# Attention keys by head, and first scores on 64-row, 32-column tiles of the array

## The chip, the cores and the metric

The kernel runs on one core of a Trainium2 chip. The metric is the device time of one execution in microseconds. Before the change its median was 1553.74 us over three runs (1549.90 to 1557.67). TensorE (PE) multiplies and transposes through a 128x128 array into PSUM (eight banks of 512 f32 columns); VectorE (DVE) and ScalarE (ACT) move and compute; SyncE (SP) and GpSimd (POOL) issue DMA.

## The reference

Three stages follow each other, over 8 batches, 8 heads, 576 tokens and a head size of 64, with 32 packed queries `p` per head:

```
p_packed = softmax(scale * p @ k.T) @ v          # first scores: 32 x 576 per head
out      = softmax(scale * q @ p_packed.T) @ p_packed
x        = heads side by side (8, 576, 512)
r, k     = sigmoid(xr @ w_r), relu(xk @ w_k) ** 2 # xr, xk: x mixed with the token before
x2       = r * (k @ w_v)
u        = x2 + (x2.T @ U @ V).T
result   = u + relu(u @ w_ch1) @ w_ch2
```

The change is in `p @ k.T`, the loads of `k` and the layouts around it.

## The kernel before

**Units.** Attention is cut into 16 units: a pair of batches (`b2` = 0, 1) times a pair of heads (`h` = 0, 1). `attention_steps` (line 634) builds one unit. A unit's keys are 2 x 576 tokens for each of two heads. `load_k` (line 591) brings, for each batch, the first 512 tokens as 128 partitions of four tokens (`p t`), and the last 64 tokens of both batches into the last 128 columns of the same tile `kin`. On a partition the order is token, head, feature, so that 128 neighbouring columns are one token of both heads.

**First scores.** Four transposes per batch turn `kin` into `kh` (row = head and feature, column = token), one more handles the tail of both batches. The packed queries of two heads are put side by side with the other head's features zeroed (`pbd`, a product with the mask `hmask`) and transposed to `pT`, so that a contraction over all 128 rows gives both heads' scores: 64 output rows per batch, in two column chunks of 288. Each of the four f32 matmuls has a stationary operand of 128 rows and 64 columns and is two MATMUL passes. The outputs of batch 0 and 1 lie on partitions 0 to 63 and 64 to 127 of one bank; the two chunks have a bank each. Two maxima, an exponential per chunk (and one per batch for the tail), and the transposes of the weights `a1` follow. Its columns are 128 per `t`.

**Order.** No order is written by hand. A planner (class `Plan`, `emit`) collects all operations with their dependencies and simulates a clock: PE and SP take, among what is ready, the lowest class and then the lowest position in the program (line 439); ACT and DVE take the lowest class and then what was ready first. A matmul of n moving columns is priced by line 203 as `f * max(f * n / 2.4, 107.0) + 3.0` ns with f = 2 for f32, whatever its tile, and at twice that where its own count of recent columns (line 202) is low (line 459). A DMA is priced at 358 GB/s if its shortest contiguous run is 512 B or more, else 180 (line 318). Attention is class 0, ahead of the matmuls of the next stages (class 1). The engines then run their queues in this order.

**Stages.** The first four units have buffers of their own, use all eight banks and are interleaved with one another, three steps apart (`LAG`, line 501), together with the casts of the first weights; their loads are issued in the order of `FIRST` (line 502). The other twelve run one after the other between the matmuls of the mixing stage (tiles `psr`, `psk`, `psv`), with two banks. The last stage (tiles `psc`) starts when the mixing stage ends.

Of the kernel before, what the change touches and what calls it, by code (L numbers as in the profile page):

```python
# [9 lines left out]
F32 = mybir.dt.float32  # L10
# [3 lines left out]
AF = mybir.ActivationFunctionType  # L14
ALU = mybir.AluOpType
# [454 lines left out]
def packed_attention_moe_mixer_kernel(  # L470
# [18 lines left out]
    B, H, S, D = q.shape  # L489
    NP = p.shape[2]  # L490
    P = 128
# [12 lines left out]
    SCALE = 1.0 / float(D) ** 0.5  # L504
# [3 lines left out]
    plan = Plan(nc)  # L508
    add, sub, mul = ALU.add, ALU.subtract, ALU.mult
# [22 lines left out]
    def ctile(name, shape, dt=F32):  # L532
        return plan.fixed(const.tile(shape, dt, name=name))

    ident = ctile("ident", [P, P])
    hmask = ctile("hmask", [P, 2, D])
# [8 lines left out]
    def ps_att():  # L545
        return plan.bank(att_banks[0], "psat", att_banks[0] is ps_a)
# [8 lines left out]
    p_t = {}  # L555

    def load_p(bp):
        t = plan.tile(p_p, [P, NJ, D], F32, "p", parts=(0, 1))
        for b2 in range(2):
            plan.dma(t.at(b2)[b2 * 64:(b2 + 1) * 64],  # L560
                     p[2 * bp + b2].rearrange("(j h) k d -> (h k) j d", h=2))
        p_t[bp] = t

    class Bufs:
# [26 lines left out]
        def load_k(self, u, after=()):  # L591
            bp, j = divmod(u, NJ)
            if u not in self.kin:
                self.kin[u] = self.tile_in("kin")
            t = self.kin[u]
            for b2 in range(2):
                src = k[2 * bp + b2, 2 * j:2 * j + 2]
                plan.dma(
                    t.at(b2)[:, b2 * 512:(b2 + 1) * 512].rearrange("p (t h d) -> p t h d", t=4, h=2),
                    src[:, 0:512, :].rearrange("h (p t) d -> p t h d", t=4), after=after)  # L600
            for b2 in range(2):
                src = k[2 * bp + b2, 2 * j:2 * j + 2]
                plan.dma(
                    t.at(2 + b2)[b2 * 64:(b2 + 1) * 64, 1024:1152].rearrange("p (h d) -> p h d", h=2),
                    src[:, 512:576, :].rearrange("h s d -> s h d"), after=after)
# [28 lines left out]
    def attention_steps(A, u, u_next):  # L634
        bp, j = divmod(u, NJ)
        kin, qin, vin = A.kin.pop(u), A.qin.pop(u), A.vin.pop(u)
        if j == 0 and bp + 1 < NBP:
            load_p(bp + 1)
        plan.tt(A.pbd, p_t[bp][:, j, :].unsqueeze(1).to_broadcast([P, 2, D]), hmask, mul)
        plain = u < NPLAIN  # L640
        kh = A.big(F32, "kh")
        qt, at = A.big(F32, "qt"), A.big(F32, "at")
        pT, ppz = A.keep(plain)
# [7 lines left out]

        if u_next is not None:
            A.kin[u_next], A.qin[u_next], A.vin[u_next] = [A.tile_in(n) for n in ("kin", "qin", "vin")]
        for b2 in range(2):
            yield
            ps = ps_att()
            for t in range(4):
                plan.transpose(ps[:, t * P:(t + 1) * P],
                               kin.at(b2)[:, b2 * 512 + t * P:b2 * 512 + (t + 1) * P], ident)
            sl = slice(b2 * 576, b2 * 576 + 512)  # L660
            plan.copy(kh[:, sl], ps)
        yield
        ps = ps_att()
        plan.transpose(ps[:, 0:P], kin[:, 1024:1152], ident)
        plan.transpose(ps[:, P:2 * P], A.pbd.rearrange("p h d -> p (h d)"), ident)
        pk_ = ps[:, 0:P].rearrange("p (b c) -> p b c", b=2)
        pp_ = ps[:, P:2 * P].rearrange("p (b c) -> p b c", b=2)
        khr = kh.rearrange("p (b c) -> p b c", b=2)[:, :, 512:576]
        plan.copy(khr, pk_)
        plan.copy(pT, pp_)  # L670
        if u_next is not None:
            A.load_k(u_next, A.after)

        st = plan.tile(A.one, [P, 16], F32, "st", parts=(0, 1))
        sps = []
        for c in range(2):
            yield
            ps = ps_att()
            for b2 in range(2):
                plan.mm(ps[b2 * 64:(b2 + 1) * 64, 0:288], pT[:, b2, :],  # L680
                        kh[:, b2 * 576 + c * 288:b2 * 576 + (c + 1) * 288],
                        start=True, stop=True, skip_group_check=True)
            plan.reduce(st[:, c:c + 1], ps[:, 0:288], ALU.max)
            sps.append(ps)
        plan.tt(st[:, 2:3], st[:, 0:1], st[:, 1:2], ALU.max)
        plan.ts(st[:, 3:4], st[:, 2:3], -SCALE, None, mul)
        a1 = A.a1
        bias = st.at(0)[:, 3:4]
        plan.act(a1[:, 0:288], sps[0][:, 0:288], AF.Exp, st.at(1)[:, 4:5], bias, SCALE)
        plan.act(a1[:, 288:512], sps[1][:, 0:224], AF.Exp, st.at(1)[:, 5:6], bias, SCALE)  # L690
        for b2 in range(2):
            r = slice(b2 * 64, (b2 + 1) * 64)
            plan.act(a1[r, 512 + b2 * 64:576 + b2 * 64], sps[1][r, 224:288], AF.Exp,
                     st.at(1)[r, 6:7], bias[r], SCALE)
        plan.reduce(st[:, 7:8], st[:, 4:7], add)
        plan.ts(st[:, 8:9], st[:, 7:8], 1e-9, None, add)
# [2 lines left out]
        for c in range(3):  # L699
            yield  # L700
            ps = ps_att()
# [3 lines left out]
            n = 3 if c < 2 else 2  # L705
# [9 lines left out]
        ps = ps_att()  # L715
# [4 lines left out]
        ps = ps_att()  # L720
# [4 lines left out]
        ps = ps_att()  # L725
        vm = vin[:, 0:1024].rearrange("p (b h t d) -> p b h t d", b=2, h=2, t=4)
        for t in range(4):
            for b2 in range(2):
                plan.mm(ps[b2 * 64:(b2 + 1) * 64, 0:P],
                        at[:, t * P + b2 * 64:t * P + (b2 + 1) * 64], vm[:, b2, :, t, :],  # L730
                        start=(t == 0), stop=False, skip_group_check=True)
# [9 lines left out]
        ps = ps_att()  # L741
# [36 lines left out]
        ps = ps_att()  # L778
# [4 lines left out]
        ps = ps_att()  # L783
        plan.transpose(ps[:, 0:P], a2g[:, 512:640], ident)
        for b2 in range(2):
            r = slice(b2 * 64, (b2 + 1) * 64)
            halves(th[r, 512:576], None if plain else tl[r, 512:576], ps[r, r])
        xo = A.big(F32, "xo", (0, 1)).rearrange("p (i b c) -> p i b c", i=NI, b=2)
        for c0, c1 in ((256, 576), (0, 256)):
# [4 lines left out]
            for n, (lh, rh) in enumerate(terms):  # L794
                for b2 in range(2):
                    r = slice(b2 * 64, (b2 + 1) * 64)
                    plan.mm(pss[b2][:, 0:w], ppz[r, lh, :], rh[r, c0:c1], start=(n == 0),
                            stop=(n + 1 == len(terms)))
# [5 lines left out]
    def attention(A, u, u_next):  # L804
        for _ in attention_steps(A, u, u_next):
            pass
# [94 lines left out]
    plan.cls = 0  # L901
    A0.after = go
    steps = [attention_steps(AX_[u], u, NJ if u == 0 else None) for u in range(NJ)]
    step = 0
    while any(s is not None for s in steps):
# [32 lines left out]
    for b2 in range(2):  # L938
        r = slice(b2 * 64, (b2 + 1) * 64)
# [5 lines left out]
    for i0, i1 in ((0, NI),):  # L945
        src = uv[:, i0 * NP:i1 * NP]
# [260 lines left out]
    def product(q, f, i, name, fresh):  # L1207

        if fresh:
            bank_abc[name] = plan.bank(ps_c1, "psc1")  # L1210
        ps = bank_abc[name][:, 0:256]
        w, x = load_ws(f, i), ops[q][i]
        n = 0
        for k in range(2):
            for wi, a in PASS:
                plan.mm(ps, half(w, wi)[:, k * P:(k + 1) * P],
                        half(x, a)[:, k * 256:(k + 1) * 256],
                        start=(fresh and n == 0), stop=(n == 5), skip_group_check=True)
                n += 1
        return ps  # L1220
# [53 lines left out]
    for n in range(len(chunks)):  # L1274
        b, c = chunks[n]
# [27 lines left out]
        if n >= CAST0:  # L1303
            plan.cls = 3
            for _ in range(len(casts) if n == NCAST else NPER):
                if casts:
                    rows, src, size, put = casts.pop(0)
# [27 lines left out]
    for q in range(NQ):  # L1335
# [11 lines left out]
        for f in range(NF):  # L1347
# [7 lines left out]
            b = product(q, f, 1, "b", True)  # L1355
# [4 lines left out]
            c = product(q, f, 2, "c", True)  # L1360
# [66 lines left out]
```

## Time and profile before

| what | value |
|---|---|
| median of three runs | 1553.74 us |
| the profiled execution's own time | 1553.02 us |
| its span, first to last instruction | 1551.2 us |
| mean granted TensorE clock | 0.986 |
| PE, PEld busy | 97%, 85% |
| DVE, ACT, POOL busy | 62%, 45%, 17% |

The times of the rows are of the one profiled execution. A MATMUL's recorded duration contains its way through the array, so that neighbours overlap in the records; how fast matmuls follow each other is read from their starts. PEld is the load of stationary operands, beside PE.

### The profile page before, as it was taken

To read this page: it belongs to the slowest core of one execution; us is meant where nothing else is said; L and a number is where in the kernel's file an instruction comes from. 1 tells how busy PE (TensorE), PEld (TensorE's weight loads), DVE (VectorE), ACT (ScalarE), POOL (GpSimd) and SP (SyncE) were. 2 spreads that over 40 slices of the span, in tenths; PEclk is the share of its full clock that TensorE was granted. 3 is DMA by queue.
4 is the path that set the end of the run, shared out by engine and by line. 5 is a ranking of instruction groups with operands and counts; after the bars stand their busy time and mean duration, and the time that the engine had idled before them with its cause. 6 is when DMAs were issued, how large, how long until landed. Compare 5 with 4: busy or idle time off the path is not lost.

```text
span 1551.2 us, 24711 instructions
## 1 busy us (share of the span) xinstructions
PE 1506.0 (97%) x8836; PEld 1311.0 (85%) x8836; DVE 964.3 (62%) x2227; ACT 705.0 (45%) x1627; POOL 270.6 (17%) x522
## 2 busy tenths in 40 slices
PE   6879899999999999999999999999999999999998
PEld 5658687888878888888899998989999999999997
DVE  5988977788887776787645354444545454443533
ACT  4867576666675666566532232222222222222221
POOL 0000000000000000001133333333333333333331
PEclk8898999999999999999999999999999999999999
DMA  9866546465554323657777867686866768676763
GB/s 200 202 175 168 155 106 170 126 184 163 158 155 142 125 92 128 240 181 241 234 211 188 215 169 224 163 239 155 234 165 180 212 168 226 162 217 157 204 171 101
DMA packets 226745, 275.59 MB, mean 178 GB/s; under 512 B 101696, under 2 KB 120448, under 8 KB 226624
## 3 DMA queue, kind: packets, MB, share of 16 engines
q0 software_dynamic: 72576, 132.15, 32.5%
q1 hardware_dynamic: 154048, 141.87, 31.5%
q8 instruction: 71, 1.16, 0.3%
q14 instruction: 50, 0.41, 0.1%
HBM read 221.45 MB, written 52.50 MB: 177 GB/s over the span
## 4 chain that ended last, share of the span: by engine, by line
PE 91%; DMA 4%; DVE 2%; ACT 2%; SPq 1%; issue 1%; DVEq 0%; ACTq 0%
PE psc L197 48%; PE psk L197 13%; PE psv L197 12%; PE psr L197 6%; PE psat L197 5%; PE psat L208 3%; SPq L311 1%; PE psu L197 1%; PE psh L197 1%; PE pst L208 1%; DMA s<-w_d 1%; DMA st<-in_moe_w_k_dram 1%; ACT a L229 1%; DMA qin<-in_q_dram 1%; DMA x_d<-xo 0%
## 5 line engine op out<-in xcount | busy, mean ns | idle before, releaser
L197 PE MATMUL psc<-w,hid 128*128 128x512 f32 x1728 | 446.5, 393 | 0.0
L197 PEld LDWEIGHTS psc<-ob,wb 128*128 128x128 f32 x3024 | 406.9, 190 | 28.3 <-ACT tmp L280 1.6
L197 PE MATMUL psc<-ob,wb 128*128 128x256 f32 x3024 | 420.9, 283 | 1.3 <-ACT tmp L280 1.3
L311 POOL DMA_DIRECT2D wb<-ws_d x504 | 267.2, 530 | 586.9 <-PE psc L197 489.7
L197 PEld LDWEIGHTS psc<-w,hid 128*128 128x128 f32 x1728 | 305.9, 189 | 50.2 <-ACT xu L280 0.2
L197 PE MATMUL psk<-xk,wk 128*128 128x384 f32 x1152 | 235.2, 345 | 1.7 <-DVE xk L250 0.9
L197 PE MATMUL psv<-wv,kk 128*128 128x512 f32 x864 | 226.8, 399 | 3.0 <-DVE wv L250 2.1
L250 DVE TENSOR_TENSOR tmp<-tmp,psc 128x256 f32<-128x256 f32 x288 | 120.7, 419 | 152.3 <-PE psc L197 141.4
L197 PEld LDWEIGHTS psk<-xk,wk 128*128 128x128 f32 x1152 | 202.6, 190 | 13.6 <-issue 3.7
L229 ACT ACTIVATE hid<-tmp 128x256 fp32r<-128x256 f32 x216 | 85.2, 416 | 248.9 <-DVE tmp L250 248.6
L197 PEld LDWEIGHTS psv<-wv,kk 128*128 128x128 f32 x864 | 157.9, 188 | 36.9 <-issue 2.8
L265 DVE SCALAR_TENSOR_TENSOR hid<-psc,hid 128x256 fp32r<-128x256 f32 x72 | 30.5, 424 | 186.4 <-ACT hid L229 186.4
L197 PE MATMUL psr<-wr,xr 128*128 128x512 f32 x432 | 111.4, 401 | 6.2 <-ACT r L280 3.0
L280 ACT ACTIVATE tmp<-psc 128x256 f32<-128x256 f32 x144 | 54.7, 380 | 137.8 <-PE psc L197 137.8
L303 POOL MEMSET x<- 128x8 f32 x4 | 0.8, 206 | 576.2 <-DVE m L262 392.0
L197 PEld LDWEIGHTS psr<-wr,xr 128*128 128x128 f32 x432 | 79.5, 189 | 25.7 <-ACT r L280 3.9
L265 DVE SCALAR_TENSOR_TENSOR hid<-tmp,hid 128x256 fp32r<-128x256 f32 x216 | 86.2, 421 | 18.0 <-ACT hid L229 12.9
L250 DVE TENSOR_TENSOR kk<-sq,kk 128x384 fp32r<-128x384 f32 x96 | 52.5, 553 | 45.3 <-ACT kk L280 43.7
L229 ACT ACTIVATE sq<-psk 128x384 f32<-128x384 f32 x96 | 46.5, 489 | 64.4 <-PE psk L197 63.4
L229 ACT ACTIVATE hid<-psc 128x256 fp32r<-128x256 f32 x72 | 27.5, 382 | 103.6 <-PE psc L197 103.6
L229 ACT ACTIVATE m<-x,om_t 128x384 f32<-128x384 f32 x96 | 57.2, 609 | 7.0 <-DVE xk L250 2.8
L262 DVE SCALAR_TENSOR_TENSOR m<-x,mu_t,m 128x384 f32<-128x384 f32 x96 | 57.9, 610 | 2.1 <-ACT m L229 1.7
(147 smaller groups left out, 1685.9 us busy)
## 6 DMA issues: line engine op xcount, KB each, us to landing
wb<-ws_d POOLq DMA_DIRECT2D x504, 256.0 KB, 3.1
st<-in_moe_w_ch_dram SPq DMA_DIRECT2D x32, 512.0 KB, 4.9
ws_d<-wb SPq DMA_DIRECT2D x56, 256.0 KB, 3.4
qin<-in_q_dram SPq DMA_DIRECT2D x32, 288.0 KB, 5.6
x_d<-xo SPq DMA_DIRECT2D x16, 576.0 KB, 3.4
x_d<-x SPq DMA_DIRECT2D x36, 256.0 KB, 3.7
u<-x_d SPq DMA_DIRECT2D x36, 256.0 KB, 5.5
out_dram<-u SPq DMA_DIRECT2D x36, 256.0 KB, 3.6
```

The source lines that it names most:

```text
L197: self.nc.tensor.matmul(o, l, r, start=start, stop=stop, **k)
L208: self.nc.tensor.transpose(out.get(), in_.get(), ident.get())
L229: self.nc.scalar.activation(o, in_.get(), func, **k)
L250: return self.elem(engs, lambda e, o, x, y: e.tensor_tensor(out=o, in0=x, in1=y, op=op), out, [a, b], self.TT, cls)
L262: ("dve",), lambda e, o, x, y, z: e.scalar_tensor_tensor(out=o, in0=x, scalar=z, in1=y, op0=op0, op1=op1), out, [a, b, s], {"dve": (1.042, ...
L265: ("dve",), lambda e, o, x, y: e.scalar_tensor_tensor(out=o, in0=x, scalar=s, in1=y, op0=op0, op1=op1), out, [a, b], self.TT, cls)
L280: self.nc.scalar.activation(o, i, AF.Copy)
L303: (self.nc.gpsimd if eng == "pool" else self.nc.vector).memset(o, 0.0)
L311: (self.nc.sync if eng == "sp" else self.nc.gpsimd).dma_start(out=o, in_=i)
```

## The change

- `load_k`: on a partition the order becomes head, token, feature. A run of 64 features (256 B) becomes one of four tokens by 64 (1 KB), in SBUF as it was in DRAM. 128 neighbouring columns are now two tokens of one head.
- `pbd` is a copy of `p` beside itself, no longer masked; the copy may go to ACT or DVE.
- The transposed keys have token parity (`r` = 0, 1) and feature as their 128 rows. The tail is transposed by head: two transposes of 64 columns into partitions 0 to 63, and copied to a tile of its own, `kt`.
- Eight f32 matmuls per unit, one for each batch, head and token parity: 64 rows by 32 columns stationary, 256 moving columns. Rows 0 to 63 write to one bank, rows 64 to 127 to the other. Four more of 64 moving columns, for the tail, use rows 0 to 63 and write behind the first bank's 256 columns.
- The maxima read 320 and 256 columns; the exponentials are one per parity with 256 columns, written in two strips of 128, and the two tails out of the first bank. `a1` has the same contents as before.
- A unit has one step (`yield`) less, as the scores are one step and no longer two.

```diff
@@ load_k
-                    t.at(b2)[:, b2 * 512:(b2 + 1) * 512].rearrange("p (t h d) -> p t h d", t=4, h=2),
-                    src[:, 0:512, :].rearrange("h (p t) d -> p t h d", t=4), after=after)
+                    t.at(b2)[:, b2 * 512:(b2 + 1) * 512].rearrange("p (h t d) -> p h t d", t=4, h=2),
+                    src[:, 0:512, :].rearrange("h (p t) d -> p h t d", t=4), after=after)
@@ attention_steps
-        plan.tt(A.pbd, p_t[bp][:, j, :].unsqueeze(1).to_broadcast([P, 2, D]), hmask, mul)
+        plan.copy(A.pbd, p_t[bp][:, j, :].unsqueeze(1).to_broadcast([P, 2, D]))
...
-            sl = slice(b2 * 576, b2 * 576 + 512)
-            plan.copy(kh[:, sl], ps)
+            plan.copy(kh[:, b2 * 512:(b2 + 1) * 512], ps)
...
-        plan.transpose(ps[:, 0:P], kin[:, 1024:1152], ident)
-        plan.transpose(ps[:, P:2 * P], A.pbd.rearrange("p h d -> p (h d)"), ident)
-        pk_ = ps[:, 0:P].rearrange("p (b c) -> p b c", b=2)
-        pp_ = ps[:, P:2 * P].rearrange("p (b c) -> p b c", b=2)
-        khr = kh.rearrange("p (b c) -> p b c", b=2)[:, :, 512:576]
-        plan.copy(khr, pk_)
-        plan.copy(pT, pp_)
+        for h in range(2):
+            plan.transpose(ps[0:64, h * P:(h + 1) * P], kin[:, 1024 + h * 64:1088 + h * 64], ident)
+        plan.transpose(ps[:, 2 * P:3 * P], A.pbd.rearrange("p h d -> p (h d)"), ident)
+        kt = plan.tile(A.one, [P, 2, P], F32, "kt")
+        plan.copy(kt[0:64], ps[0:64, 0:2 * P].rearrange("p (h c) -> p h c", h=2))
+        plan.copy(pT, ps[:, 2 * P:3 * P].rearrange("p (b c) -> p b c", b=2))
...
-        sps = []
-        for c in range(2):
-            yield
-            ps = ps_att()
-            for b2 in range(2):
-                plan.mm(ps[b2 * 64:(b2 + 1) * 64, 0:288], pT[:, b2, :],
-                        kh[:, b2 * 576 + c * 288:b2 * 576 + (c + 1) * 288],
-                        start=True, stop=True, skip_group_check=True)
-            plan.reduce(st[:, c:c + 1], ps[:, 0:288], ALU.max)
-            sps.append(ps)
+        yield
+        sps = [ps_att() for _ in range(2)]
+        for b2 in range(2):
+            for h in range(2):
+                o = slice(b2 * 64 + h * 32, b2 * 64 + (h + 1) * 32)
+                for r in range(2):
+                    rows = slice(r * 64, (r + 1) * 64)
+                    plan.mm(sps[r][o, 0:256], pT[rows, b2, h * 32:(h + 1) * 32],
+                            kh[rows, b2 * 512 + h * 256:b2 * 512 + (h + 1) * 256],
+                            start=True, stop=True, skip_group_check=True)
+        for b2 in range(2):
+            for h in range(2):
+                o = slice(b2 * 64 + h * 32, b2 * 64 + (h + 1) * 32)
+                plan.mm(sps[0][o, 256:320], pT[0:64, b2, h * 32:(h + 1) * 32],
+                        kt[0:64, h, b2 * 64:(b2 + 1) * 64], start=True, stop=True, skip_group_check=True)
+        plan.reduce(st[:, 0:1], sps[0][:, 0:320], ALU.max)
+        plan.reduce(st[:, 1:2], sps[1][:, 0:256], ALU.max)
...
-        plan.act(a1[:, 0:288], sps[0][:, 0:288], AF.Exp, st.at(1)[:, 4:5], bias, SCALE)
-        plan.act(a1[:, 288:512], sps[1][:, 0:224], AF.Exp, st.at(1)[:, 5:6], bias, SCALE)
+        for r in range(2):
+            plan.act(a1[:, 0:512].rearrange("p (n r c) -> p n r c", n=2, r=2)[:, :, r, :],
+                     sps[r][:, 0:256].rearrange("p (n c) -> p n c", n=2), AF.Exp,
+                     st.at(1)[:, 4 + r:5 + r], bias, SCALE)
...
-            plan.act(a1[r, 512 + b2 * 64:576 + b2 * 64], sps[1][r, 224:288], AF.Exp,
+            plan.act(a1[r, 512 + b2 * 64:576 + b2 * 64], sps[0][r, 256:320], AF.Exp,
```

## Rows read from the trace of the kernel before

**Rows 1.** The page: busy time and DMA packets of the whole run.
```profile
PE 1506.0 (97%) x8836; PEld 1311.0 (85%) x8836; DVE 964.3 (62%) x2227; ACT 705.0 (45%) x1627; POOL 270.6 (17%) x522
...
DMA packets 226745, 275.59 MB, mean 178 GB/s; under 512 B 101696, under 2 KB 120448, under 8 KB 226624
```

**Rows 2.** The page: the chain that ended last, by engine.
```profile
PE 91%; DMA 4%; DVE 2%; ACT 2%; SPq 1%; issue 1%; DVEq 0%; ACTq 0%
```

**Rows 3.** Busy us of each engine (instructions) by stretch; clock, DMA share, GB/s.
```profile
0.00:50.00 50.00, 36.18 (x201) 26.69 (x202) 31.24 (x86) 27.98 (x76) 1.32 (x11) 0.86 0.97 204
50.00:110.00 60.00, 48.38 (x271) 36.32 (x269) 52.24 (x137) 42.46 (x106) 0.00 (x0) 0.86 0.69 183
110.00:200.00 90.00, 79.46 (x444) 62.46 (x443) 78.72 (x192) 61.27 (x147) 0.00 (x0) 0.94 0.61 159
200.00:500.00 300.00, 297.60 (x1723) 246.96 (x1724) 240.39 (x578) 197.71 (x452) 0.60 (x2) 1.00 0.54 148
500.00:1551.00 1051.00, 1044.42 (x6203) 938.59 (x6201) 561.67 (x1238) 375.55 (x849) 268.66 (x509) 1.00 0.66 186
```

**Rows 4.** Score MATMULs: whole run, 200 to 500, 110 to 200 us.
```profile
L197 PE MATMUL psat<-kh,pT x128: 406/406/742, 8.4 to 465.4; 128*64 128x288 f32 x128
...
L197 PE MATMUL psat<-kh,pT x64: 406/406/457, 204.6 to 465.4; 128*64 128x288 f32 x64
...
L197 PE MATMUL psat<-kh,pT x24: 406/406/667, 110.5 to 171.6; 128*64 128x288 f32 x24
```

**Rows 5.** PE in order of time around the last unit's scores.
```profile
464.57 1.19 PE L197 MATMUL psat<-kh,pT 128*64 128x288 f32 x8
465.69 0.50 PE L197 MATMUL psv<-wv,kk 128*128 128x512 f32 x1
```

**Rows 6.** The same scores alone by stretch: PE, PEld, DVE, ACT.
```profile
464.57:464.86 0.29, 0.29 (x3) 0.19 (x4) 0.00 (x0) 0.00 (x0) 1.00 0.67 205
464.86:465.10 0.24, 0.24 (x4) 0.14 (x2) 0.00 (x0) 0.00 (x0) 1.00 0.97 175
```

**Rows 7.** PE in order of time around a product of 64-row tiles.
```profile
47.84 0.81 PE L197 MATMUL psat<-th,ppz 64*128 64x320 f32 x4
48.58 0.49 PE L197 MATMUL psat<-ppt,qt 128*128 128x128 f32 x2
```

**Rows 8.** PE in order of time around a value product.
```profile
474.23 1.51 PE L197 MATMUL psat<-vin,at 128*64 128x128 f32 x18
475.49 0.42 PE L197 MATMUL psk<-xk,wk 128*128 128x384 f32 x1
```

**Rows 9.** PE in order of time around a unit's key transposes.
```profile
461.51 1.03 PE L208 MATMUL psat<-ident,kin 128*128 128x128 f32 x8
462.30 0.95 PE L197 MATMUL psk<-xk,wk 128*128 128x384 f32 x4
```

**Rows 10.** Groups of ACT (whole run) and DVE work (up to 110 us).
```profile
L280 ACT ACTIVATE kh<-psat 128x128 f32<-128x128 f32 x12 | 3.3, 279 | 1.9 <-PE psat L208 1.5 <-DVE pT L283 0.2
L280 ACT ACTIVATE xo<-psat 128x256 f32<-128x256 f32 x19 | 7.2, 386 | 9.0 <-PE psat L197 8.9
...
L265 DVE SCALAR_TENSOR_TENSOR st<-a,st 128x512 f32<-128x512 f32 x12 | 8.2, 686 | 4.6 <-ACT a L229 4.6
```

**Rows 11.** DMA of the first 50 us: packets, transfers with their time to landing.
```profile
DMA packets 25064, 10.22 MB, mean 204 GB/s; under 512 B 22320, under 2 KB 24368, under 8 KB 25061
...
kin<-in_k_dram SPq DMA_DIRECT2D x8, 256.0 KB, 4.5
...
vin<-in_v_dram SPq DMA_DIRECT2D x8, 256.0 KB, 4.6
```

**Rows 12.** SP's issues in order of time.
```profile
7.74 5.17 SPq L311 DMA_DIRECT2D kin<-in_k_dram  x4
12.96 2.51 SPq L311 DMA_DIRECT2D vin<-in_v_dram  x4
```

More of the change, by code (lines that the diff above doesn't have):

```diff
@@ L656, in attention_steps @@
             ps = ps_att()
-            for t in range(4):
-                plan.transpose(ps[:, t * P:(t + 1) * P],
-                               kin.at(b2)[:, b2 * 512 + t * P:b2 * 512 + (t + 1) * P], ident)
-            sl = slice(b2 * 576, b2 * 576 + 512)
-            plan.copy(kh[:, sl], ps)
+            for n in range(4):
+                plan.transpose(ps[:, n * P:(n + 1) * P],
+                               kin.at(b2)[:, b2 * 512 + n * P:b2 * 512 + (n + 1) * P], ident)
+            plan.copy(kh[:, b2 * 512:(b2 + 1) * 512], ps)
         yield
         ps = ps_att()
-        plan.transpose(ps[:, 0:P], kin[:, 1024:1152], ident)
-        plan.transpose(ps[:, P:2 * P], A.pbd.rearrange("p h d -> p (h d)"), ident)
-        pk_ = ps[:, 0:P].rearrange("p (b c) -> p b c", b=2)
-        pp_ = ps[:, P:2 * P].rearrange("p (b c) -> p b c", b=2)
-        khr = kh.rearrange("p (b c) -> p b c", b=2)[:, :, 512:576]
-        plan.copy(khr, pk_)
-        plan.copy(pT, pp_)
+        for h in range(2):
[4 more added lines that the diff above has]
+        plan.copy(pT, ps[:, 2 * P:3 * P].rearrange("p (b c) -> p b c", b=2))
         if u_next is not None:
```

## The prediction

> **What bounds the kernel now.** I read the page's shares first [rows 1]: TensorE is busy 97% of the span, VectorE 62%, ScalarE 45%. The chain of waits says the same from its end: 91% of it is PE [rows 2]. The table by stretches [rows 3] shows where that holds. From 200 to 500 us PE is busy 297.6 of 300 us, after 500 us 1044 of 1051. Before 110 us it is not the bound: PE is busy 36.2 of 50 us and then 48.4 of 60 us, at a mean granted clock of 0.86, while the DMA engines are at 0.97 of their time up to 50 us and VectorE is busy 52.2 of 60 us after that. From 110 to 200 us PE reaches 79.5 of 90 us.
>
> So an attention unit (16 of them) is worth something different by its place. The first-score matmuls are 128 instructions, eight to a unit; 64 of them (8 units) fall into 200 to 500 us, 24 (3 units) into 110 to 200 us [rows 4], and the other 40 (5 units) before. In the eight late units every array nanosecond counts whole; in the three middle ones at 79.5/90 = 0.88; in the first five a shorter chain counts, not array time.
>
> **First scores, before.** One unit in the dense stretch: its eight MATMULs of 288 columns start at 464.57 us and the next group (psv) at 465.69, a slot of 1.12 us [rows 5]. The stretch of 0.24 us inside it holds four MATMUL records [rows 6], two that end and two that begin: the eight run as four rounds of two, a round taking 0.24 us, and the first 0.29. That is 0.29 + 3 x 0.24 = 1.01 us of array; the rest, 0.11, is the changeover. The two of a round are the two column halves of the array (b2 = 0 and 1). Row halves do it too: four passes of 320 columns on two row tiles, each 0.24 x 320/288 = 0.27 us, take the slot 47.84 to 48.58 [rows 7], 0.74 us and not 1.07.
>
> **First scores, after.** Eight matmuls of 64 rows, 32 columns and 256 moving columns on eight different tiles, then four of 64 columns on the four tiles of the upper row half; 24 MATMULs for 8, as each f32 matmul is two passes. A pass of 256 columns is 0.24 x 256/288 = 0.213 us, one of 64 is 0.053.
> - All eight tiles side by side: 2 x 0.213 + 2 x 0.053 = 0.53 us, with the same 0.05 for the first round 0.58, against 1.01: -0.43 per unit.
> - Only two at a time, as the rows show: 8 x 0.213 + 4 x 0.053 + 0.05 = 1.97 us: +0.95 per unit.
> - Instructions limited by their own flow: the densest run in the trace is 18 MATMULs of the value product from 474.23 to 475.49, 1.26/18 = 0.07 us each [rows 8]; 24 would take 1.68 us against 1.12: +0.56. But that run streams 128 columns in pairs, so it is at the array's own limit and the figure is an upper bound.
>
> I take -0.35: in the rows a tile's second pass doesn't hold back the other tile's first one, and nothing in them stops at two; 0.08 is kept for filling eight tiles with weights.
>
> The Trainium skill speaks against this. "TensorE: Matmul & The Clock Gate", section "Part 3: Packing small matmuls — row/col tiling", holds that matmuls start and end strictly in program order. By it, the second pass of each matmul would block the next tile: four matmuls of two passes in the old unit would need five rounds, 5 x 0.24 = 1.20 us, and the new unit nine rounds of 0.213 and about five of 0.053, 2.2 us, so +1.0 per unit. The trace shows four rounds and not five [rows 6], so the rule does not hold for two tiles here; that it could for eight is part of the first rival below. The same section gives a 16-tile product 10.6 times a single one's rate, which no run here shows.
>
> **Transposes.** Eight of the keys stay; the tail's one becomes two of 64 columns. Eight from 461.51 to 462.30 are 0.79/8 = 0.10 us each [rows 9]. One more: +0.1 (bounds 0 and +0.3, if the narrower one costs a changeover like the 0.11 above).
>
> **Copies and exponentials.** The tail copy goes from 128x128 (279 ns on ScalarE) to 64x256 (386 ns for 128x256): +0.11 us. The masked product of p becomes a copy of the same size that either engine may take. The maxima read 576 columns in all before and after, the exponentials 512 and the two tails: same sums. The two copies' rows are in [rows 10]. From 200 us on VectorE has 60 of 300 us free and ScalarE 102 [rows 3], so these cost nothing there; in the start they would be 0.1 us a unit. One thing moves: the bank of the lower half is now free only after the second exponential and the other after the fourth, so the first query transposes get a bank some 0.6 us later. Other matmuls fill PE from 200 us on; before 110 us all eight banks serve attention.
>
> **Key loads.** The bytes stay, but a partition's run in SBUF grows from 256 B to 1 KB. In the first 50 us 22,320 of 25,064 packets are under 512 B, and the engines move 204 GB/s at 0.97 busy, 210 at full; after 500 us, with large packets, it is 186 at 0.66, 282 at full [rows 3, 11]. The eight main key transfers of the first four units (256 KB each, 2.1 MB) would go from 10.0 to 7.4 us: -2.6 us at most. Against it, a value transfer that already has the new shape lands no sooner (4.6 us against 4.5 for keys) [rows 11], so the lower bound is 0. SP's second group of key issues takes 5.17 us, the values behind it, in the new shape, 2.51 [rows 12]. I take -2.0, near the rate's end, as the engines are full there; later loads are early enough to be hidden.
>
> **Sum.** Eight late units (-0.35 + 0.10) x 8 = -2.0; three middle ones -0.25 x 3 x 0.88 = -0.7; the start -2.0 for the loads and about -1.0 for five score chains (bounds 0 and -2.2, five times the -0.43; a maximum that ran beside the second chunk now stands behind all matmuls, so I take less than half). Together -5.7 us on this execution's 1553.0 us (span 1551.2 and 1.8 around it): 1547.3, and as the median of the runs shown is 0.7 above, 1547.5. The 0.37% is less than the 0.5% that a measurement of this kernel can tell from no change.
>
> **Rivals.**
> *Two tiles at a time.* Only what the trace shows goes side by side. Then +0.95 + 0.10 for each late and middle unit, 8 x 1.05 + 3 x 1.05 x 0.88 = +11.2, and in the start five longer score chains, about +1, less the loads' -2.0: +10, 1564. With x more per unit the change is 10.6 x - 1.0 (8 and 3 x 0.88 units): slower than before from 0.1 us on, by over 0.5% from 0.83 on. For it: no row has more than two tiles at once. Against: the old work had no more than two tiles to offer, so the rows can't show a limit.
>
> *The planner's price.* The order on every engine is written by a list planner that prices an f32 matmul as two passes of at least 107 ns each, 2n/2.4 ns for n columns, plus 3, whatever its tile. The scores go from 4 x 483 = 1.93 us to 8 x 430 + 4 x 217 = 4.3 us in its clock (twice that where it believes the clock low, as in the start), while the chip needs less. So attention's ScalarE and VectorE work comes later in its order and weight casts get in front. A cast is seven VectorE operations of at most 0.69 us [rows 10], so up to 4.8 us. If two or three of them slip in front of the four first units, the dense stretch begins 8 to 14 us later; half of it comes back, as the casts must be done anyway: +5 on the forecast, about 1552.5, no change. For it: VectorE is 87% busy from 50 to 110 us. Against: from 200 us on PE's fill is not tight, 2.4 us idle in 300.
>
> *A better start.* Loads and score chains move the whole start: of the first 110 us PE is idle for 25, and the clock at a mean of 0.86 costs some 15 more [rows 3]. If a fifth of these 40 comes back, -8 more: 1539. For it: by `FIRST` the second unit's query is issued on SP behind those key loads, which hold SP for 5.17 us [rows 12]. Against: after 50 us VectorE sets the pace, with unchanged work.
>
> **How the numbers follow.** Forecast 0.50, two tiles 0.20, planner 0.20, better start 0.10. The forecast's own range is 1541 to 1554. Faster by over 0.5% (below 1546) is 0.4 of the forecast's 0.50, all of the better start, none of the rest: 0.30. Slower by over 0.5% (above 1561.5) is 0.7 of the two-tile case and 0.15 of the planner's: 0.17. The rest, 0.53, is no change. The range 1538 to 1564 leaves out about half of the two-tile case above and, below, half of the better start and the edge of the forecast, together some 0.18.
>
> **What would show it.** Right: in the dense stretch the slot from the first score MATMUL to the next group is about 0.75 us with 24 records in it, stretches of 0.21 us holding many more than four; PE total from 200 to 500 us carries the same MoE matmuls in less time; the packets under 512 B, 101,696 of the run [rows 1], fall by some 32,800 (32 main key transfers of 1024); the second key group on SP issues in less than 4 us [rows 12]. Wrong: a slot of 1.5 us or more (two tiles or an instruction limit); a start whose first psr group comes later than before; PE idle over 5 us between 200 and 500 us (a planner that is ahead of the chip).

## The result, and the profile after

The changed kernel takes 1563.25 us (median of six runs, 1560.83 to 1564.21) against 1554.08 us in the same comparison: ratio 1.0057, 95% interval 1.0040 to 1.0074. The forecast was 1547.5 us, with a range of 1538 to 1564. The kernel became slower by some 9 us where it was to become faster by 6.

What the chip does in one unit went as forecast. The page of the changed kernel, against [rows 1, 2]:

```profile
span 1561.1 us, 25249 instructions
...
PE 1504.0 (96%) x9108; PEld 1309.4 (84%) x9108; DVE 966.2 (62%) x2223; ACT 709.9 (45%) x1633; POOL 269.2 (17%) x522
...
DMA packets 202171, 275.63 MB, mean 177 GB/s; under 512 B 68928, under 2 KB 95872, under 8 KB 202048
...
PE 87%; DVE 5%; DMA 4%; ACT 2%; issue 1%; SPq 1%; DVEq 0%; ACTq 0%
```

The packets under 512 B fell by 32,768. PE's busy time is 2.0 us less, yet the span is 9.9 us more, so PE waits 11.9 us longer; in the chain of waits 4 points of the span went from PE, and 3 came to VectorE. The stretches say where, against [rows 3] (same columns):

```profile
0.00:50.00 50.00, 31.14 (x252) 24.58 (x253) 32.32 (x83) 28.43 (x76) 1.31 (x11) 0.83 0.95 218
50.00:110.00 60.00, 45.82 (x268) 33.02 (x268) 50.53 (x135) 38.47 (x103) 0.00 (x0) 0.80 0.60 164
110.00:200.00 90.00, 81.55 (x513) 65.04 (x512) 79.39 (x189) 63.17 (x148) 0.00 (x0) 0.94 0.60 164
200.00:500.00 300.00, 291.26 (x1818) 241.81 (x1817) 239.40 (x573) 194.49 (x439) 0.23 (x2) 1.00 0.52 151
500.00:1561.00 1061.00, 1054.25 (x6265) 944.93 (x6263) 564.55 (x1246) 385.36 (x871) 267.67 (x509) 1.00 0.65 184
```

Up to 110 us PE idles 33.0 us instead of 25.4, and the mean clock is 0.81, not 0.86. From 200 to 500 us PE idles 8.7 us instead of 2.4. The last attention unit ends later now, so the comparisons below take 200 to 560 us: first before, then after.

```profile
200.00:560.00 360.00, 357.08 (x2017) 300.20 (x2018) 287.68 (x669) 237.61 (x527) 0.60 (x2) 1.00 0.51 145
```

```profile
200.00:560.00 360.00, 349.70 (x2119) 291.33 (x2117) 283.62 (x664) 236.70 (x521) 0.23 (x2) 1.00 0.50 147
```

Idle is the length less the PE column: 2.9 us, and now 10.3. So 7.4 of the 11.9 us that PE waits longer lie in this dense stretch. Another 5.5 lie ahead of it: up to 200 us PE idles 41.5 us instead of 36.0. There its waits for keys have grown; up to 110 us (in total, times, longest), before and after:

```profile
PE psat L208 <- DMA kin<-in_k_dram: 5.6, 2, 4.3
```

```profile
PE psat L208 <- DMA kin<-in_k_dram: 12.7, 4, 3.7
```

**The scores themselves.** The new unit in the dense stretch, in PE's order of time, against [rows 5]:

```profile
301.56 0.66 PE L197 MATMUL psat<-kh,pT 64*32 64x256 f32 x16
302.01 0.31 PE L197 MATMUL psat<-kt,pT 64*32 64x64 f32 x8
302.25 2.35 PE L197 MATMUL psr<-wr,xr 128*128 128x512 f32 x9
304.44 1.98 PE L197 MATMUL psv<-wv,kk 128*128 128x512 f32 x8
307.44 0.55 PE L208 MATMUL psat<-ident,qin 128*128 128x128 f32 x3 [1.01 <-ACT a L229]
```

From 301.56 to 302.25 the slot is 0.69 us with 24 records; it was 1.12 with 8. The same records by stretch, against [rows 6]:

```profile
301.56:301.80 0.24, 0.24 (x9) 0.18 (x17) 0.00 (x0) 0.00 (x0) 1.00 0.00 0
301.80:302.01 0.21, 0.21 (x16) 0.14 (x4) 0.00 (x0) 0.00 (x0) 1.00 0.01 4
```

In 0.21 us, one pass of 256 columns, sixteen records lie: eight that end and eight that begin. All eight tiles run side by side. The mean slot of the late units is 0.70 us.

**What comes after them.** The last row of PE above waits 1.01 us for ScalarE: three query transposes want a bank that the exponentials of these scores still hold. ScalarE's first exponential, with its wait, and VectorE's work at that time:

```profile
306.36 0.47 ACT L229 ACTIVATE a<-psat,st 128x256 f32<-128x256 f32 x1 [3.60 <-DVE st L256]
```

```profile
302.80 0.70 DVE L265 SCALAR_TENSOR_TENSOR st<-a,st 128x512 f32<-128x512 f32 x1
303.41 0.69 DVE L250 TENSOR_TENSOR m<-m,a 128x512 f32<-128x512 f32 x1
304.01 0.42 DVE L256 TENSOR_SCALAR a<-st 128x512 int32<-128x512 int32 x1
304.46 0.69 DVE L265 SCALAR_TENSOR_TENSOR a<-st,a 128x512 int32<-128x512 int32 x1
305.07 0.81 DVE L269 TENSOR_REDUCE st<-psat 128x1 f32<-128x320 f32 x2
```

The scores are there at 302.25. VectorE then does four operations of a weight cast, because they stand before the maxima in its written order, and comes to the maxima at 305.07. The kernel before, in the same place of a unit (its scores begin at 351.02), has one operation between its two maxima and none ahead of them:

```profile
351.78 0.45 DVE L269 TENSOR_REDUCE st<-psat 128x1 f32<-128x288 f32 x1
352.15 0.41 DVE L256 TENSOR_SCALAR a<-st 128x512 int32<-128x512 int32 x1
352.48 0.45 DVE L269 TENSOR_REDUCE st<-psat 128x1 f32<-128x288 f32 x1
```

Counted from the timelines for the eight units from 200 us on, the operations that begin between the start of the last score and the second maximum were 1, 1, 1, 2, 1, 1, 1, 1 before and are 8, 6, 4, 2, 0, 6, 7, 3 after. From that start to the end of the maxima it is 1.4 us a unit on average before, and 3.7 after. PE's waits from 200 to 560 us (in total, times, longest) put 5.9 us of the idle time on that bank; before, this wait does not occur there:

```profile
PE psat L208 <- ACT a L229: 5.9, 7, 1.3
```

### The profile page after: what moved, and what is told of

Its sections match the earlier page's. It is cut to its first block, busy times and chain, and to the rows that moved or that the text cites. A ratio compares the mean times of both kernels' runs of the same rounds, so it can differ in the third digit from the quotient of the medians.

```text
span 1561.1 us, 25249 instructions
## 1 busy us (share of the span) xinstructions
PE 1504.0 (96%) x9108; PEld 1309.4 (84%) x9108; DVE 966.2 (62%) x2223; ACT 709.9 (45%) x1633; POOL 269.2 (17%) x522
## 4 chain that ended last, share of the span: by engine, by line
PE 87%; DVE 5%; DMA 4%; ACT 2%; issue 1%; SPq 1%; DVEq 0%; ACTq 0%
PE psc L197 48%; PE psk L197 12%; PE psv L197 12%; PE psr L197 6%; PE psat L197 4%; PE psat L208 3%; PE psh L197 1%; PE pst L208 1%; ACT a L229 1%; PE psu L197 1%; DVE m L250 1%; DMA st<-in_moe_w_v_dram 1%; SPq L311 1%; DMA s<-w_d 1%; DMA x<-x_d 1%
## 5 line engine op out<-in xcount | busy, mean ns | idle before, releaser
L197 PE MATMUL psr<-wr,xr 128*128 128x512 f32 x432 | 115.0, 408 | 3.8 <-ACT xr L280 2.3
L265 DVE SCALAR_TENSOR_TENSOR hid<-tmp,hid 128x256 fp32r<-128x256 f32 x216 | 86.2, 422 | 17.8 <-ACT hid L229 12.7
```

The costliest lines, as they stand in the source:

```text
L197: self.nc.tensor.matmul(o, l, r, start=start, stop=stop, **k)
L265: ("dve",), lambda e, o, x, y: e.scalar_tensor_tensor(out=o, in0=x, scalar=s, in1=y, op0=op0, op1=op1), out, [a, b], self.TT, cls)
```

## The experiments

Two prices of the planner that move with this change are tested. One was a rival of the prediction: the scores rise from 1.93 to 4.3 us a unit in its clock. The other was not seen there: the price of a DMA asks at line 318 whether the shortest run is at least 512 B; the key loads now pass that test, so their price falls from 256 KB at 180 GB/s to 256 KB at 358. In the expectations, the planner's theory (P) is that these prices and not the chip's work cost the time, at first by PE's waits for keys in the start; against it stand theories by which the work itself (tiles, transposes, loads) or the start does. All ratios below are to the kernel before, timed on the same chip in the same batch, with their 95% interval.

**1. The score price alone, on either kernel.** An optional price is put into `mm`; the chip's work stays, only the order written for it changes.

```
-    def mm(self, out, lhsT, rhs, start, stop, **k):
+    def mm(self, out, lhsT, rhs, start, stop, price=None, **k):
-            return f * max(f * n / 2.4, 107.0) + 3.0
+            return price or f * max(f * n / 2.4, 107.0) + 3.0
 # scores: a_true price=60.0 / 25.0 (tail): 0.58 us a unit; a_same 200.0 / 83.0: 1.93 us
 # scores of the kernel before: b_dear price=1077.0: 4.3 us a unit; b_true 253.0: 1.01 us
```

> The changed kernel, with the planner's price of its twelve score matmuls set so that a unit's sum is 1.93 us in the planner's clock as before the change (200 ns for each of 256 columns, 83 for each of 64), in place of 4.3 us; the chip's work is the changed kernel's. Theory P (the price writes an order in which TensorE waits for key loads ahead of attention's own next step): 1546 to 1550 us, 0.3 to 0.5% below the kernel before, key waits of PE before 110 us back to about 6 us. Rival W (the changed work itself costs the time: loads by head, two tail transposes, later banks, one step fewer): stays at 1560 to 1565. Rival N (any new order moves the time by several us without a rule): anywhere between 1548 and 1565.

> The changed kernel with the planner's price of the score matmuls near what the chip shows (60 ns and 25 ns, 0.58 us a unit). Theory P: as fast as with the old sum or faster, 1543 to 1550 us. Rival W: 1560 to 1565. Rival N: 1548 to 1565, and not near the run with the old sum.

> The kernel before, with nothing changed but the planner's price of its four score matmuls, 1077 ns each in place of 483 (4.3 us a unit, what the changed kernel's matmuls are priced at). Theory P: slower than before by more than the changed kernel is, as the gain of the tiles is missing: 1563 to 1572 us, with key waits of PE before 110 us above 10 us. Rival W: 1554, as the work is the old one. Rival N: 1550 to 1562.

> The kernel before with the price of its score matmuls near what the chip shows (253 ns each, 1.01 us a unit, in place of 1.93). Theory P: 1549 to 1556 us, since a price below the old one moves no wait in front of a ready step. Rival W: 1554. Rival N: it scatters, 1546 to 1562.

Measured: a_same 1554.49 us (0.9996, 0.9980 to 1.0013); a_true 1548.34 (0.9953, 0.9937 to 0.9969); b_dear 1572.19 (1.0102, 1.0075 to 1.0128); b_true 1553.67 (0.9983, 0.9965 to 1.0001). So the price of 4.3 us slows the kernel before too, whose chip work is untouched, by 1.0%; its PE idles 9.4 us from 200 to 560 us, against 2.9:

```profile
200.00:560.00 360.00, 350.58 (x2004) 292.06 (x2005) 283.59 (x669) 232.05 (x522) 0.23 (x2) 1.00 0.51 142
```

Another 12.7 us of idle time come up to 200 us (48.7 against 36.0), so there the start loses more than the dense stretch. With the price near what the chip needs, a_true, the changed kernel idles 1.3 us from 200 to 560 us:

```profile
200.00:560.00 360.00, 358.66 (x2187) 305.01 (x2187) 288.78 (x678) 242.57 (x525) 0.40 (x2) 1.00 0.49 142
```

and VectorE's first maximum waits only for the scores, which end at 293.69 in this unit:

```profile
292.81 0.69 DVE L265 SCALAR_TENSOR_TENSOR a<-st,a 128x512 int32<-128x512 int32 x1
293.86 0.49 DVE L269 TENSOR_REDUCE st<-psat 128x1 f32<-128x320 f32 x1 [0.36 <-PE psat L197]
```

The waits for keys up to 110 us went as theory P had it: 6.5 us in a_same (about 6 expected), 14.1 in b_dear (above 10), and 4.5 in a_true. The time did not follow in a_same, which missed its expectation by over 4 us. Its dense stretch is mended (idle 3.2 us), and up to 110 us it idles 26.6 us, nearly as before; but its mean clock there is 0.76.

```profile
0.00:110.00 110.00, 83.40 (x519) 60.73 (x519) 81.34 (x215) 67.54 (x178) 1.31 (x11) 0.76 0.74 188
```

**2. Where the score price does its harm.** Theory S: in the start, where the prediction had put it. Theory D: in the dense stretch. One kernel gets the low price of a_true in the first four units alone, the other in the twelve others alone.

```
 # a_start
-  price=60.0                          # tail: 25.0
+  price=60.0 if u < NJ else None      # tail: 25.0 if u < NJ else None
 # a_dense
+  price=None if u < NJ else 60.0      # tail: None if u < NJ else 25.0
```

> The changed kernel with the low price (60 and 25 ns) for the score matmuls of the four first units alone; the other twelve keep the changed kernel's price (4.3 us a unit). Theory S (the price does its harm in the start, where TensorE is put behind key loads): close to the run with the low price everywhere, 1548 to 1552 us. Theory D (the harm is in the dense stretch, where TensorE then waits for exponentials it believes done): close to the changed kernel, 1558 to 1563. Both by halves: 1553 to 1557.

> The same the other way round: the four first units at the changed kernel's price, the other twelve at the low one. Theory S: 1559 to 1563 us. Theory D: 1548 to 1552. Both by halves: 1553 to 1557.

Measured: a_start 1563.87 us (1.0047, 1.0030 to 1.0064), a_dense 1554.03 (0.9985, 0.9969 to 1.0001). With the twelve others dear, the low price in the first four units gives nothing back; in the other twelve it gives back 10 us. a_dense lies in the range that stood for both by halves, above that of theory D, and by the ratios 0.32% (5 us) above a_true: once the twelve are cheap, the price of the first four costs time too. The wait that goes with that price is the one for keys, 5.6 us up to 110 us in a_start and 12.3 in a_dense; yet a_start's idle time up to 110 us is no less for it (34.9 us, 33.0 in the changed kernel). PE from 200 to 560 us, first a_start (idle 11.1), then a_dense (3.1):

```profile
200.00:560.00 360.00, 348.89 (x2105) 290.33 (x2104) 281.30 (x660) 235.48 (x514) 0.23 (x2) 1.00 0.50 145
```

```profile
200.00:560.00 360.00, 356.94 (x2154) 301.63 (x2154) 284.22 (x660) 237.39 (x528) 0.22 (x2) 1.00 0.50 143
```

So the larger part of the harm in the changed kernel is in the dense stretch, as theory D has it; theory S alone falls.

**3. A curve of prices.** Same edit, other numbers: a_040 41/18 (0.40 us a unit), a_077 80/33 (0.77), a_130 135/55 (1.3), a_290 300/125 (2.9), and on the kernel before b_290 with 725 (2.9).

> The changed kernel with a price of 0.40 us a unit for the scores (41 and 18 ns), below what the chip takes (about 0.6). If the harm comes only from a price above the chip's time: 1547 to 1553 us, and TensorE idle from 200 to 560 us below 4 us, as in the runs at 0.58, 0.77 and 1.93. If any wrong price harms: above 1554.

> The changed kernel with a price a third above the low one (80 and 33 ns, 0.77 us a unit): nearly the same price, another order. It tells how far an order alone moves the time. If the price rules: 1546 to 1551 us, as with 0.58. If orders scatter (theory N): more than 4 us away from that run's 1548.3.

> The same at 1.3 us a unit (135 and 55 ns), between 0.77 and 1.93. Theory D (a dear score makes the planner fill VectorE with casts ahead of the maxima): 1550 to 1554 us, idle from 200 to 560 us 2 to 4 us. If orders alone scatter by 10 us: anywhere up to 1563.

> The same at 2.9 us a unit (300 and 125 ns), between 1.93 and 4.3. Theory D: between the two, 1554 to 1561 us, idle from 200 to 560 us 5 to 9 us, since two to four of the casts' operations stand before the maxima. If the harm is a matter of one bad order at 4.3: 1548 to 1555.

> The kernel before at a price of 2.9 us a unit (725 ns each), between its 1.93 and the 4.3 that took 1572 us. Theory D: 1557 to 1567 us, idle from 200 to 560 us 4 to 8 us. If it was one bad order: 1551 to 1557.

Measured, with PE's idle time from 200 to 560 us in the profiled run:

```
price a unit   after: us, ratio (interval)              idle    before: us, ratio          idle
0.40           1548.38  0.9952 (0.9936 to 0.9968)        3.1
0.58           1548.34  0.9953 (0.9937 to 0.9969)        1.3
0.77           1551.70  0.9971 (0.9954 to 0.9988)        2.5
1.01                                                             1553.67  0.9983            2.4
1.3            1552.52  0.9981 (0.9970 to 0.9993)        2.0
1.93           1554.49  0.9996 (0.9980 to 1.0013)        3.2     1                          2.9
2.9            1555.71  1.0002 (0.9991 to 1.0013)        3.7     1563.62  1.0049            4.2
4.3            1563.25  1.0057 (1.0040 to 1.0074)       10.3     1572.19  1.0102            9.4
```

There are three misses. a_077 lies 0.7 us above its range. a_290 idles 3.7 us in the dense stretch, not 5 or more, and b_290, with a time and an idle time in its ranges, has not lost its 8 us there but up to 110 us, where PE idles 38.0 us against 25.4:

```profile
0.00:110.00 110.00, 72.02 (x422) 52.13 (x423) 80.03 (x214) 62.35 (x167) 1.32 (x11) 0.84 0.80 188
```

So only at 4.3 us does the dense stretch break. Below that it idles 1.3 to 4.2 us, and after 560 us PE idles 4.5 to 6.6 us in every one of these kernels; what else differs between them lies in the first 200 us, in idle time and clock.

**4. Honest prices for the other small products too.** a_all is a_true with the value product at 112 ns a matmul and the last product at half its price.

```
 # value product: price=112.0
 # last product:
+  price=(2.0 if plain else 1.0) * w / 2.4 / (1.0 if plain else 2.0) + 3.0
```

> The low price for the scores, and two more products priced as the chip runs them side by side: the value product on two column halves (112 ns for each of 217) and the last product on two row halves (half of its price). If the planner's error about tiles is worth time wherever it stands: 1542 to 1547 us. If only the scores' error of 2.4 us more was harmful: 1547 to 1550.

Measured 1556.55 us (1.0003, 0.9986 to 1.0020), 8 above a_true and well above what was expected. Its dense stretch is as good (idle 1.7 us); it lost from 110 to 200 us, where PE idles 13.8 us against 8.2 in a_true:

```profile
110.00:200.00 90.00, 76.16 (x490) 60.07 (x488) 77.03 (x191) 58.51 (x142) 0.00 (x0) 0.94 0.58 154
```

A price nearer the chip's time does not of itself write a better start.

**5. The key loads' price.** a_dma is a_true with the key loads priced at 180 GB/s again, the transfers unchanged. a_step is a_true with one more `yield` ahead of the tail's matmuls.

```
-    def dma(self, out, in_, cls=None, after=(), eng="sp"):
+    def dma(self, out, in_, cls=None, after=(), eng="sp", short=False):
-            return ... / (358.0 if min(runs) >= 512 else 180.0)
+            return ... / (358.0 if min(runs) >= 512 and not short else 180.0)
 # load_k, the two main loads: short=True
```

> The changed kernel at the low price of the scores (0.58 us a unit), its key loads in the new shape but priced by the planner at 180 GB/s as before, in place of 358. If the load's price puts key work too early in TensorE's order: idle up to 110 us back to 25 to 28 us from 30, and 1543 to 1547 us. If not: 1547 to 1552 and idle of 30 or more.

> The changed kernel at the low price with the step given back that a unit lost (a yield ahead of the tail's matmuls). If the four interleaved units need it: idle up to 110 us below 27 us and 1543 to 1547 us. If not: within 1.5 us of the run without it, 1547 to 1550.

Measured: a_dma 1540.49 us (0.9913, 0.9900 to 0.9926), the best of all kernels here and below its range; it idles 28.2 us up to 110 us. a_step took 1549.53 (0.9962, 0.9950 to 0.9973), an interval that overlaps that of a_true. By the names in the two traces, a_step has a_true's order on every engine, so the step changed nothing and the two times show what one order scatters. a_dma's gain pointed to a second harmful price. Theory L says so; theory N says that any new order moves the start by some us either way. Four more kernels: the price alone on the kernel before (b_358, `long=True` forces 358), the price of 180 on the changed kernel with scores at 4.3 us (a_dma43) and at 1.93 us (a_dma19, where both prices are those of before), and the new load alone (b_load):

```
 # b_load: the kernel before with
-  t.at(b2)[...].rearrange("p (t h d) -> p t h d", t=4, h=2), src[...].rearrange("h (p t) d -> p t h d", t=4), after=after)
+  t.at(b2)[...].rearrange("p (h t d) -> p h t d", t=4, h=2), src[...].rearrange("h (p t) d -> p h t d", t=4), after=after, short=True)
```

> The kernel before, chip work unchanged, the planner alone prices the key loads at 358 GB/s as it does after the change. Theory L (too cheap a load brings the transposes forward in the order, PE waits for keys at the start): +4 to +10 us, PE idle before 110 us over 30 (before 25.4). Theory N (any new order moves the start by some us, in either direction): within 4 us of before, idle before 110 us 24 to 30.

> The changed kernel, scores priced at 4.3 us as in it, key loads priced at 180 GB/s, chip work unchanged. Theory L: 1553 to 1558, the harm of the score price (PE idle 8 to 11 us from 200 to 560 us) stays, the start gains 5 to 9. Theory N: 1560 to 1566, or a shift of any sign below 4 us.

> The changed kernel, scores priced at 1.93 us (as before the change), key loads at 180 GB/s: both of the planner's prices are those of before, the chip work is that of after. Theory L: 1544 to 1549, below 1554.5 of the same kernel with loads at 358 by 6 to 10. Theory N: 1550 to 1558. It is also the change's chip work with no price changed; the forecast for that was 1547.5.

> The kernel before with the new key loads (1 KB runs) and nothing else: key loads priced at 180 GB/s as before, so every engine's order is that of before to the instruction; its transposes are left as they were and read the tokens in another order, so the output is not the reference's. This is the chip's side of the load alone. Forecast's step: -2.0 us (0 to -2.6). If the loads give nothing on the chip, within 1 us of before. If the start passes more on than the loads themselves (a clock that rises earlier), -4 or more.

Measured: b_358 1547.18 us (0.9946, 0.9928 to 0.9965): the same false price that was thought harmful makes the kernel before faster, which neither theory had (+4 us or more, or within 4 us); up to 110 us it idles 31.4 us, as theory L had it, and is faster all the same. a_dma43 1565.76 (1.0060, 1.0038 to 1.0083): no gain from the price of 180 there. a_dma19 1546.73 (0.9940, 0.9922 to 0.9958). b_load 1547.55 (0.9948, 0.9929 to 0.9968). Raising the load price's rate from 180 to 358 thus gives -0.54% on the kernel before, +0.40% and +0.56% on the changed one with scores at 0.58 and 1.93 us, and -0.03% at 4.3. Theory L falls: one change of the price has either sign, so its effect goes with the whole order that it writes. a_dma19 alone lies in that theory's range. The score price keeps its sign in all three pairs of 1.93 and 4.3 us: +1.02% (before, 180), +0.61% (after, 358), +1.20% (after, 180); and a_dma43 idles 8.5 us in the dense stretch where a_dma19 idles 2.2. The wait for the exponentials' bank is 5.9 us in the one and 0.6 in the other; PE's waits from 200 to 560 us in a_dma43, then its stretch and that of a_dma19:

```profile
PE psat L208 <- ACT a L229: 5.9, 5, 1.6
```

```profile
200.00:560.00 360.00, 351.50 (x2144) 294.38 (x2143) 287.32 (x678) 234.06 (x513) 0.22 (x2) 1.00 0.50 145
```

```profile
200.00:560.00 360.00, 357.78 (x2164) 302.93 (x2163) 293.12 (x677) 235.33 (x522) 0.23 (x2) 1.00 0.52 149
```

## Why the prediction was wrong

**The account.** With both prices kept, the changed chip work, with the order written for it, is worth -9.1 us (a_dma19 against its batch's 1555.83). The load price then takes back 0.56% of 1554, +8.7, and the score price 0.61%, +9.5: +9.1 in all, measured +9.2. The three steps lead from one kernel to the other, so that they add up proves nothing; each has an uncertainty of some 3 to 4 us. The other way round it is -9.1, +18.6 for the score price and -0.5 for the load price. The prices are not additive, but either way round the score price alone takes back about the whole gain or more.

**The sum itself.** The prediction's terms add up to 1547.3 us, and with the 0.7 that it puts on top to 1548.0, not 1547.5. The slip changes nothing below.

**First scores: right.** -0.42 us a unit, at the lower bound of -0.43 (taken: -0.35). The two-tile rival is out.

**Transposes: right.** Taken was 0.1 us for one more. The tail's two 64-column transposes start at 291.35 and are followed at 291.57 (a_true, PE in order of time), 0.11 us each:

```profile
291.35 0.38 PE L208 MATMUL psat<-ident,kin 128*64 128x128 f32 x2
291.57 0.27 PE L208 MATMUL psat<-ident,pbd 128*128 128x128 f32 x1
```

**Key loads: the direction is right, the size is not.** SP's issues against [rows 12]:

```profile
6.98 2.24 SPq L311 DMA_DIRECT2D kin<-in_k_dram  x4
9.27 3.00 SPq L311 DMA_DIRECT2D vin<-in_v_dram  x4
```

The second key group takes 2.24 us instead of 5.17. The prediction took -2.0 us (0 to -2.6) for the loads; b_load, with every engine's order as before, gained 8.3 (5 to 11 by its interval), more than the bound. The rate does not give it: in b_load's first 50 us the engines move 211 GB/s at 0.92 busy, 229 at full against 210 before, by which the prediction's 2.1 MB would save 0.8 us, and a key transfer lands in 4.3 us instead of 4.5. The profiled run of b_load was the longest of its seven, so where the rest comes from is not shown. Its runs go from a span of 1542.8 us at a mean clock of 0.993 to 1553.6 at 0.985, and their mean clock is 0.989 against 0.985 for the 13 runs of the kernel before in that batch; 0.4% of 1550 us is 6, so the clock in the start is a likely carrier, not a shown one. One run of the changed kernel took 1564.21 us at 0.933, where the others took 1560.83 to 1563.74 at 0.979 to 0.989, so the mean clock does not always carry time. Since b_load alone gains about what a_dma19 gains, the scores' own share of the time can't be told from the scatter of orders; it stays open.

**Copies and exponentials at nothing: failed in this order.** "Other matmuls fill PE from 200 us on" was the cover for the later bank. In the changed order it was not there: PE waited 5.9 us for just these banks. In a_true, with the same chip work, it was there again.

**The step that failed: the weight given to the planner's price.** The forecast's sum has it at nothing. The rival named the mechanism, casts in front of attention on VectorE, and then put it into the start and argued it away from the dense stretch: "from 200 us on PE's fill is not tight, 2.4 us idle in 300". That row shows the opposite. PE's 297.6 of 300 us was reached by an order in which one operation stands between scores and maxima; a full engine is the achievement of that order, not a slack that survives another. b_dear does the same work on the chip in another order and idles 9.4 us from 200 to 560 us, not 2.9. The rival's 5 us on the forecast should have been about 10 to 19, by the two ways round above. The start that it named has its part too, though by waits for keys (5.6 us before, 12.7 after) and not by the casts that it argued with. And line 318, which the prediction passed over although it weighed the same loads, made a second rewrite of the start.

**The better start.** The chance of 0.10 went to a start that gives back 8 us more. b_load gained 6 us more than the forecast's loads, and a_dma is 14 us under before with 1540.49; but which of the orders get it could not be read from the profile of before. The 15 us that the clock was to cost in the start are read too low, as the clock column misses the first 16.6 us (see the last section).

**What would have shown it.** The list at the end of the prediction held the right sign: PE idle over 5 us between 200 and 500 us (it is 8.7). A second sign of being wrong came too: the first psr group begins at 75.3 us and not 65.2. But it begins at 77.6 in a_dma, the fastest kernel, so it says little of the time. The lines for being right, slot, packets and SP's issues, all came out and say nothing of the time.

## What to carry to other kernels

Where a planner writes the order, first work out what every edit does to its prices: an edit that makes an operation cheaper on the chip and dearer in the plan can lose more than it gains. A test is to give the old kernel the new price. Price a tiled matmul by the tiles that run together, then time more than one order: here a_dma, with such a price, beats both kernels at 1540.49 us, but 8 us of that came with the order that one more price wrote, which nothing here could foretell: a kernel with two more products priced near the chip's time came to 1556.55. An engine that is full says that its order fits, not that it can bear another.

## What was not expected of the hardware

Twelve f32 matmuls of two passes each on 64-row, 32-column tiles took 0.70 us, with sixteen records inside one pass's 0.21 us. The Trainium skill ("TensorE: Matmul & The Clock Gate", section "Part 3: Packing small matmuls — row/col tiling") has matmuls start and end strictly in program order; by it, if the two passes of each matmul are issued one behind the other, this unit would have grown by the prediction's 1.0 us, and the trace has it shrink by 0.42. All eight first passes begin within 0.05 us, ahead of all eight second ones. The trace doesn't show the order of issue, so either that order is not matmul by matmul or the rule doesn't hold for f32 passes on different tiles.

The clock in the start is a cost of its own. It moves with the order and also between executions of one order. The profiled executions of a_true and a_step, with one order, idle 38.3 and 35.0 us up to 200 us; the second, which idles less, has the lower mean clock there (0.85 and 0.80) and the longer span, 1554.3 us against 1548.3. By the rows up to 200 us, the time at the lower level, which is half the higher, is twice the clock's shortfall times the length: 2 x 0.14 x 110 + 2 x 0.06 x 90 = 42 us in the kernel before, and 39 in a_dma, whose rows are these:

```profile
0.00:110.00 110.00, 81.85 (x586) 62.86 (x587) 89.18 (x234) 73.41 (x188) 1.31 (x11) 0.84 0.82 208
110.00:200.00 90.00, 81.37 (x511) 64.82 (x509) 81.02 (x195) 64.38 (x154) 0.00 (x0) 0.98 0.55 147
```

a_same's row above gives 2 x 0.24 x 110 = 53 us for its first 110 us alone. All these figures are too low, as the column does not have the whole start. In the changed kernel it has 1.00 (2.4 GHz) up to 20 us, and 0.57, near the lower level of 1.2 GHz, from 20 to 25 us:

```profile
15.00:20.00 5.00, 2.03 (x10) 1.55 (x8) 4.93 (x11) 3.06 (x8) 0.00 (x0) 1.00 1.23 223
20.00:25.00 5.00, 2.08 (x27) 1.11 (x27) 2.81 (x9) 2.94 (x11) 0.00 (x0) 0.57 1.09 277
```

That looks like a fall behind a late query, for which PE waits 3.58 us from 17.03 us on. But TensorE's own rows show no fall:

```profile
12.53 1.09 PE L208 MATMUL psat<-ident,kin 128*128 128x128 f32 x4 [3.40 <-DMA kin<-in_k_dram]
20.61 0.83 PE L208 MATMUL psat<-ident,qin 128*128 128x128 f32 x3 [3.58 <-DMA qin<-in_q_dram]
26.02 1.09 PE L208 MATMUL psat<-ident,kin 128*128 128x128 f32 x4 [3.34 <-DMA kin<-in_k_dram]
36.90 0.60 PE L208 MATMUL psat<-ident,kin 128*128 128x128 f32 x4
```

The groups behind the first, third and fourth of these rows begin at 13.41, 26.90 and 37.34 us. So a transpose takes 0.22 us ahead of the wait, as long as behind it at 0.50, and 0.11 later at 1.00: PE already ran at the lower level before the wait, and the column's 1.00 there is not its clock. The trace's first clock record begins at 17.3 us here, at 16.6 in the kernel before, at 13.9 in a_dma and at 32.1 in a_dense, and a stretch without a record counts as 1.00. A mean clock of the start is thus to be read beside the rate of PE's own rows. What a late query costs by the clock is not shown.
